# A fused transformer block, rebuilt: P as the stationary operand, scores over four row groups, engine lists from a planner

## Chip, cores, metric

One Trainium2 chip, one core. The metric is device time in microseconds (us), lower is better. A ratio compares a kernel's runs with those of the kernel before in the same rounds on the same chip, so it is not quite the ratio of the medians that are quoted. The kernel before ran in every set of rounds, with medians of 1544.6 to 1547.1 us, so medians of different sets can be compared to about 0.2%.

## The reference

Batch 1, 2048 tokens (S), width 1024 (D), 32 heads of 32 that share one K and one V, a gated FFN of width 3584, all inputs bf16:

```python
h  = x + softmax((LN(x) @ wq) @ (LN(x) @ wk).T / sqrt(32)) @ (LN(x) @ wv) @ wo   # per head; K and V shared
h2 = h + (sigmoid(LN(h) @ w_gate) * (LN(h) @ w_up)) @ w_down
```

The scores alone are 32 x 2048 x 2048 numbers, and each has to go through one exp on ScalarE (ACT).

## The kernel before

Queries are worked in 8 blocks of 256. Inside a block there are 8 quads of 4 heads, and for each quad 16 steps, one for each 128 keys. A step computes scores transposed (keys on partitions, 4 heads x 256 queries in two PSUM banks), ACT takes the exp of all 1024 columns, and P V accumulates with V and a block of ones as stationary operands over four column groups. The FFN of the block before is background work, put into fixed slots: two steps (a "unit" below) at a time.

Some words: P is the exp of the scores. A matmul's stationary operand (`lhsT`) is held in TensorE's 128x128 array while the other (`rhs`) moves past it. A row group is 32 of the array's rows, as many as a head is wide (`32*128` in the traces), and a column group 32 of its columns (`128*32`). Going from such a matmul to one over the whole array (`128*128`), or back, is a change of tiling. A PSUM bank holds 512 f32 columns; the program shares out eight of them.

```python
S_ps = psum_tensor("S_ps", [P, 4, 512])    # two score buffers of two banks
OL_ps = psum_tensor("OL_ps", [P, 2, 512])  # P V and row sums: two banks
F_ps = psum_tensor("F_ps", [P, 2, 512])    # all other matmuls: two banks
# ... cut ...
def quad_heads(q):                         # two tiles of Q^T, two row groups
    p_, lohi = q // 2, q % 2
    ta, tb = 2 * p_, 2 * p_ + 1
    rgx, rgy = (0, 1) if lohi == 0 else (2, 3)
    return [(ta, rgx), (tb, rgx), (ta, rgy), (tb, rgy)]

def pe_st(i):                              # scores of step i
    # ... waits cut, but for this one:
    if i >= 2: c_exp.wait(pe, i - 1)       # the buffer's exp, two steps ago
    for (j, bank, half) in [(0, 0, 0), (2, 1, 0), (1, 0, 1), (3, 1, 1)]:
        tile, rg = hq[j]
        pe.matmul(S_ps[:, 2 * buf + bank, half * QC:(half + 1) * QC],
                  lhsT=kT4[DH * rg:DH * (rg + 1), kt * P:(kt + 1) * P],
                  rhs=QT[DH * rg:DH * (rg + 1), tile, qc * QC:(qc + 1) * QC],
                  start=True, stop=True, tile_position=(DH * rg, 0))

def pe_pv(i):
    c_exp.wait(pe, i + 1)
    for j in range(4):                     # row sums
        pe.matmul(OL_ps[DH * j:DH * (j + 1), ob, QC:2 * QC], lhsT=ones,
                  rhs=Pring[:, slot, j * QC:(j + 1) * QC], tile_position=(0, DH * j), ...)
    for j in range(4):                     # V
        pe.matmul(OL_ps[DH * j:DH * (j + 1), ob, 0:QC], lhsT=V_sb[:, kt, :],
                  rhs=Pring[:, slot, j * QC:(j + 1) * QC], tile_position=(0, DH * j), ...)

# main loop, once in two steps (MACRO = 2); the exps of both steps stand on ACT
for i2 in range(jm - MACRO, jm):
    pe_pv(i2)
    if steps[i2][2] == KT - 1: dve_groupnorm(i2 // KT)
bg_step(cur_budget[0] * MACRO)             # FFN, projections: a fixed share of the block's work
for i2 in range(jm + MACRO, jm + 2 * MACRO):
    pe_st(i2)
```

The softmax here doesn't subtract the row's maximum and nothing guards it: scores larger than these inputs give would overflow.

## Time and profile before

| | before |
|---|---|
| median | 1544.52 us (3 runs, 1541.85 to 1546.78); a fourth, in the rounds with the kernel after, took 1552.20 |
| first exp starts, last exp ends | 64.0 us, 1426.4 us |
| behind the last exp | 118 us |
| distance of every second exp start (one unit): median, mean | 2.49 us, 2.66 us |

The page of the kernel before: busy time by engine, then busy tenths in 40 slices of the span.

```profile
span 1544.6 us, 38302 instructions
PE 1410.1 (91%) x17622; PEld 803.1 (52%) x17736; DVE 388.6 (25%) x686; ACT 1078.2 (70%) x1277; POOL 61.7 (4%) x117
...
PE   4799999999999999999999999999899999999678
...
ACT  2588886777687776877687776777688777777010
```

TensorE (PE) is busy in nearly every slice, ACT is not. The costliest groups of the same page (line, engine, operation, tiles, shapes, count, busy us, mean ns, idle time just before and who ended it):

```profile
L634 ACT ACTIVATE arena<-S_ps 128x1024 bf16<-128x1024 f32 x1024 | 1010.0, 1025 | 292.4 <-PE S_ps L624 291.5
...
L624 PE MATMUL S_ps<-arena 32*128 32x256 bf16 x4096 | 340.0, 280 | 22.9 <-ACT arena L634 20.7
L647 PE MATMUL OL_ps<-arena 128*32 128x256 bf16 x4096 | 275.1, 288 | 0.0
L653 PE MATMUL OL_ps<-arena 128*32 128x256 bf16 x4096 | 271.5, 285 | 0.0
```

ACT stands idle for 291.5 us because scores (L624) are not there. The timeline of one unit (start, duration, engine, line and so on; several instructions are merged in one line):

```profile
703.03 0.61 PE L624 MATMUL S_ps<-arena 32*128 32x256 bf16 x8
703.49 1.94 ACT L634 ACTIVATE arena<-S_ps 128x1024 bf16<-128x1024 f32 x2 [0.56 <-PE S_ps L624]
...
703.57 0.29 PE L647 MATMUL OL_ps<-arena 128*32 128x256 bf16 x4
...
703.69 0.28 PE L653 MATMUL OL_ps<-arena 128*32 128x256 bf16 x4
...
703.80 0.28 PE L647 MATMUL OL_ps<-arena 128*32 128x256 bf16 x4
...
703.91 0.28 PE L653 MATMUL OL_ps<-arena 128*32 128x256 bf16 x4
...
704.12 1.47 PE L274 MATMUL F_ps<-arena 128*128 128x512 bf16 x6
...
705.52 0.28 PE L624 MATMUL S_ps<-arena 32*128 32x256 bf16 x2
```

Read it as one turn of 2.49 us: scores at 703.03, two exps (1.94 us), P V, FFN, the next scores at 705.52. TensorE runs through, ACT waits 0.56 us a turn. A stretch of one block of 256 queries (busy time by engine, clock, share of DMA) says the same:

```profile
core 0: us, PE busy (x) PEld busy (x) DVE busy (x) ACT busy (x) POOL busy (x), PEclk, DMA share, GB/s
575.00:746.00 171.00, 160.56 (x2094) 92.58 (x2102) 39.97 (x67) 129.12 (x155) 3.06 (x6) 0.97 0.35 94
```

### The profile page before, as it was taken

The page shows a single profiled execution, that of the slowest core. Times are in us where ns is not written, and L with a number is a line of the kernel's source. Part 1 is how long each engine was busy: PE and PEld are TensorE (multiplying, and loading weights), DVE is VectorE, ACT ScalarE, POOL GpSimd, SP SyncE. Part 2 cuts the span into 40 slices and gives each one's busy share as a digit, 9 for nine tenths or more (in the row PEclk, how much of TensorE's full clock was granted, in tenths as well). Part 3 has the DMA queues.
Part 4 walks back from the last instruction along what each step waited for, and adds up shares of the span by engine and source line. Part 5 has one row for each costly group of instructions (what it writes and reads, how often), then busy time and mean ns, then how long its engine had stood idle before and what let it go on. Part 6 is the DMA issues. An engine that isn't in the chain of part 4 may idle for free.

```text
span 1544.6 us, 38302 instructions
## 1 busy us (share of the span) xinstructions
PE 1410.1 (91%) x17622; PEld 803.1 (52%) x17736; DVE 388.6 (25%) x686; ACT 1078.2 (70%) x1277; POOL 61.7 (4%) x117
## 2 busy tenths in 40 slices
PE   4799999999999999999999999999899999999678
PEld 2444336654466446654466445654466446654464
DVE  7433122211322123211322123211322123211311
ACT  2588886777687776877687776777688777777010
POOL 6200100000000000000000000000000000000000
PEclk9899768999899999999899999999899999999899
DMA  4500504550155204550155203550155204550371
GB/s 152 157 2 1 192 15 111 137 138 12 45 145 158 62 22 110 137 137 12 45 139 160 66 19 107 144 137 12 45 138 163 64 8 111 138 137 11 88 216 41
DMA packets 246417, 144.36 MB, mean 93 GB/s; under 512 B 5281, under 2 KB 238753, under 8 KB 246257
## 3 DMA queue, kind: packets, MB, share of 16 engines
q1 hardware_dynamic: 243712, 132.14, 31.1%
q0 software_dynamic: 2544, 9.77, 1.8%
q8 instruction: 139, 2.28, 0.6%
q14 instruction: 22, 0.17, 0.0%
HBM read 137.69 MB, written 4.19 MB: 92 GB/s over the span
## 4 chain that ended last, share of the span: by engine, by line
PE 74%; DMA 6%; DVE 6%; issue 6%; ACT 6%; POOL 1%; SPq 0%; POOLq 0%; DVEq 0%
PE F_ps L274 42%; PE S_ps L624 16%; PE OL_ps L647 8%; DMA arena<-in_B_w_up_dram 6%; PE OL_ps L653 6%; ACT arena L634 4%; DVE st L385 2%; DVE arena L844 2%; ACT tnh L839 2%; PE F_ps L446 1%; PE F_ps L520 1%; DVE arena L423 1%; POOL dsb L403 0%; DMA arena<-in_A_x_dram 0%; SPq L699 0%
## 5 line engine op out<-in xcount | busy, mean ns | idle before, releaser
L634 ACT ACTIVATE arena<-S_ps 128x1024 bf16<-128x1024 f32 x1024 | 1010.0, 1025 | 292.4 <-PE S_ps L624 291.5
L274 PE MATMUL F_ps<-arena 128*128 128x256 bf16 (+1 forms) x4866 | 778.2, 306 | 68.7 <-DVE arena L844 27.3
L274 PEld LDWEIGHTS F_ps<-arena 128*128 128x128 bf16 x4976 | 448.8, 99 | 335.0 <-issue 124.8
L624 PE MATMUL S_ps<-arena 32*128 32x256 bf16 x4096 | 340.0, 280 | 22.9 <-ACT arena L634 20.7
L647 PE MATMUL OL_ps<-arena 128*32 128x256 bf16 x4096 | 275.1, 288 | 0.0
L653 PE MATMUL OL_ps<-arena 128*32 128x256 bf16 x4096 | 271.5, 285 | 0.0
L624 PEld LDWEIGHTS S_ps<-arena 32*128 32x128 bf16 x4096 | 145.4, 93 | 223.4 <-ACT arena L634 150.8
L844 DVE SCALAR_TENSOR_TENSOR arena<-tnh,F_ps 128x256 bf16<-128x256 f32 x224 | 94.2, 421 | 618.6 <-ACT tnh L839 618.3
L647 PEld LDWEIGHTS OL_ps<-arena 128*32 128x32 bf16 x4096 | 109.7, 97 | 119.4 <-issue 115.7
L839 ACT ACTIVATE tnh<-F_ps 128x256 f32<-128x256 f32 x224 | 84.8, 379 | 105.8 <-PE F_ps L274 105.8
L667 DVE RECIPROCAL rL<-OL_ps 128x256 f32<-128x256 f32 x64 | 112.2, 1753 | 141.5 <-PE OL_ps L653 141.5
L653 PEld LDWEIGHTS OL_ps<-arena 128*32 128x32 bf16 x4096 | 111.6, 99 | 3.3
L886 DVE SCALAR_TENSOR_TENSOR arena<-F_ps,arena 128x512 bf16<-128x512 f32 x32 | 22.1, 691 | 209.5 <-PE F_ps L274 209.5
L446 PE MATMUL F_ps<-arena 128*128 128x128 bf16 x256 | 28.6, 280 | 39.5 <-DVE arena L423 38.9
L399 POOL TENSOR_SCALAR zb<-mvb 128x1 bf16<-128x1 bf16 x32 | 10.7, 334 | 1261.7 <-DVE mvr L394 1261.7
L446 PEld LDWEIGHTS F_ps<-arena 128*128 128x128 bf16 x256 | 21.4, 126 | 47.2 <-DVE arena L423 36.1
L741 DVE TENSOR_TENSOR arena<-F_ps,arena 128x512 bf16<-128x512 f32 x32 | 22.1, 691 | 87.9 <-PE F_ps L274 87.9
L385 DVE BATCH_NORM_STATS2 st<-arena 128x6 f32<-128x512 bf16 x64 | 40.9, 681 | 5.2 <-DMA arena<-in_A_x_dram 5.2
L504 DVE CAST arena<-F_ps 128x512 bf16<-128x512 f32 x30 | 20.7, 690 | 74.5 <-PE F_ps L274 71.0
L454 ACT ACTIVATE arena<-F_ps 128x1024 bf16<-128x1024 bf16 x16 | 16.1, 1025 | 27.2 <-PE F_ps L446 27.2
L672 DVE TENSOR_TENSOR arena<-OL_ps,rL 128x256 bf16<-128x256 f32 x64 | 27.1, 424 | 2.2
L403 POOL TENSOR_TENSOR dsb<-zb,smallb 128x1 bf16<-128x1 bf16 x32 | 23.2, 724 | 2.7
(30 smaller groups left out, 127.9 us busy)
## 6 DMA issues: line engine op xcount, KB each, us to landing
arena<-in_B_w_gate_dram SPq DMA_DIRECT2D x112, 512.0 KB, 3.9
arena<-in_B_w_up_dram SPq DMA_DIRECT2D x112, 512.0 KB, 5.3
arena<-in_A_x_dram SPq DMA_DIRECT2D x32, 256.0 KB, 2.7
arena<-in_B_w_down_dram POOLq DMA_DIRECT2D x4, 1792.0 KB, 16.2
out_dram<-arena SPq DMA_DIRECT2D x32, 128.0 KB, 1.7
arena<-in_A_wq_dram POOLq DMA_DIRECT2D x1, 2048.0 KB, 10.6
arena<-in_A_wo_dram SPq DMA_DIRECT2D x32, 64.0 KB, 1.9
arena<-in_A_wk_dram POOLq DMA_DIRECT2D x4, 64.0 KB, 4.2
```

Source lines behind the costliest of these rows:

```text
L274: last = pe.matmul(out_bank_ap, lhsT=lhsT, rhs=rhs, start=start, stop=stop)
L385: ins_ = dve.bn_stats(st[:, sslot, c, :], src[:, c * 512:(c + 1) * 512])
L403: ins_ = pool.tensor_tensor(out=dsb[:, t:t + 1], in0=zb[:, t:t + 1], in1=halfb_ap, op=ALU.pow)
L446: ins_ = pe.transpose(out=tpv[:, dt * P:(dt + 1) * P], in_=src[:, dt * P:(dt + 1) * P], identity=ident)
L624: ins_ = pe.matmul(S_ps[:, 2 * buf + bank, half * QC:(half + 1) * QC], lhsT=kT4[DH * rg:DH * (rg + 1), kt * P:(kt + 1) * P], rhs=QT[DH * r ...
L634: ins_ = act.activation(out=Pring[:, slot, :].rearrange("p (a b) -> p a b", a=2), in_=S_ps[:, 2 * buf:2 * buf + 2, :], func=ACTF.Exp, scal ...
L647: ins_ = pe.matmul(OL_ps[DH * j:DH * (j + 1), ob, QC:2 * QC], lhsT=ones, rhs=Pring[:, slot, j * QC:(j + 1) * QC], start=(kt == 0), stop=Fa ...
L653: ins_ = pe.matmul(OL_ps[DH * j:DH * (j + 1), ob, 0:QC], lhsT=V_sb[:, kt, :], rhs=Pring[:, slot, j * QC:(j + 1) * QC], start=False, stop=( ...
L667: ins_ = dve.reciprocal(rL[:, ob, :], OL_ps[:, ob, QC:2 * QC])
L672: ins_ = dve.tensor_tensor(out=OT[:, qc % 2, q, :], in0=OL_ps[:, ob, 0:QC], in1=rL[:, ob, :], op=ALU.mult)
L839: ins_ = act.activation(out=tnh[:, k % 2, :], in_=F_ps[:, b, 0:256], func=ACTF.Tanh, scale=0.5)
L844: ins_ = dve.scalar_tensor_tensor(out=hactT[:, ft, :], in0=tnh[:, k % 2, :], scalar=1.0, in1=F_ps[:, b, 256:512], op0=ALU.add, op1=ALU.mult)
```

## The change

The intent: take work from TensorE and keep ACT fed.

- P V: P becomes the stationary operand (128 keys x 128 queries), V and a ones column (33 columns) move past it. One group does all 16 key blocks of 4 heads in a row, so its output can share the two general banks, and the row-sum matmuls go.
- The two banks thus freed become a third score buffer (six banks).
- A score "visit" is 512 keys x 128 queries x 4 heads: 16 matmuls of 128 columns over four row groups, two exps behind it. It holds as many scores as a unit before, and there are 512 of both.
- A planner, run while the program is built, simulates the engines with assumed costs and fixes the order of each engine's list; FFN, projections and P V fill the time between visits.
- x is loaded whole and scores start with the first keys; the first layer norm (LN) centres on DVE and scales on DVE or ACT; Q goes through DRAM; four slabs of gate/up weights instead of two.

```diff
-        S_ps = EC(nc.psum_tensor("S_ps", [P, 4, 512], F32))
-        OL_ps = EC(nc.psum_tensor("OL_ps", [P, 2, 512], F32))
+        S_ps = EC(nc.psum_tensor("S_ps", [P, 6, 512], F32))
         F_ps = EC(nc.psum_tensor("F_ps", [P, 2, 512], F32))
@@ scores: pe_st() goes, emit_S() comes (cut) @@
+            deps = [q_ready[c][g], k_ev[2 * kq], k_ev[2 * kq + 1]]
+            if 2 * v - 2 >= 0:
+                deps.append(exps[2 * v - 2])
+            for kk in range(KB):
+                for j in range(4):
+                    kt = kq * KB + kk
+                    bank = 2 * ((2 * v + j // 2) % NB) + j % 2
+                    last = pl.op("pe", mm(S_ps[:, bank, kk * P:(kk + 1) * P], kT4[DH * j:DH * (j + 1), kt * P:(kt + 1) * P],
+                                          QTb[DH * j:DH * (j + 1), c % 2, g, qo:qo + P], True, True,
+                                          tile_position=(DH * j, 0)),
+                                 deps if (kk == 0 and j == 0) else [], occ=15.0, lat=15.0 + 170.0 + SEM)
@@ P V: pe_pv() goes, mk_PV() comes (cut) @@
+                for j in range(4):
+                    for kt in range(NT):
+                        r.append((mm(F_ps[:, b, j * VS:j * VS + DH + 1], Pr[:, slot, co:co + P], Vaug[:, kt, 0:DH + 1],
+                                     kt == 0, kt == NT - 1), DH + 1, []))
@@ the planner's choice (cut) @@
+                run = max(pl.free["act"], t) + sum(o.occ for o in pl.heap["act"])
+                can_s = sd is not None and known(sd, t)
+                if can_s and run - t < 750.0:
+                    emit_S(v)
@@ first LN (cut) @@
+            xcent[t] = pl.op("dve", lambda t=t: DVE.tensor_scalar(
+                out=x_sb[:, t, :], in0=x_sb[:, t, :], scalar1=mvr[:, 0, t, 0:1], scalar2=None, op0=ALU.subtract), ...)
+            xnorm[t] = evac(lambda: ACT.activation(out=dst, in_=src, func=ACTF.Copy, scale=sc),
+                            lambda: DVE.tensor_scalar(out=dst, in0=src, scalar1=sc, scalar2=None, op0=ALU.mult), ...)
```

## The prediction

> **What bounds the kernel now.** TensorE. Cut into eight windows of 171 us from 62 to 1430 us (busy time by windows), each has PE busy about 161 us (94%) and ACT about 130 us (76%). The timeline at 700 us shows the repeating unit, two score steps in 2.49 us: 8 score matmuls (about 0.54 us), 16 column-tiled P V and row-sum matmuls (about 0.55 us), FFN or projection matmuls (12 of 256 columns: 1.42 us, where 12 x 0.109 us = 1.3 us would do), and PE idle at three changes of array tiling (0.16 to 0.2 us where shown). ACT does two exps in 1.94 us and then waits 0.56 us for scores; one exp lasts 1.02 us, two in a row start 0.92 us apart. A window has 64 such units, so 2.67 us each with the larger stalls (output projection, layer norm, tanh to multiply).
> Outside: scores start at 63.6 us, after a first layer norm paced by DVE (2.76 us per tile); after the last exp (1426.4 us) comes 118 us, in which gate/up waits on weight DMA about 1 us for every slab (15 us), and 12 us go to projection and 6 us to norm bubbles.
>
> **What changes, per unit (512 in both).**
> - P V: P becomes the stationary operand, 33 columns move (V and a ones column), so the row-sum matmuls go. Still 16 matmuls. The V projection in the trace has this very form (128x128 weights, 32 columns): 32 in 0.95 us, 25 ns each when the clock is full. The Trainium skill, "TensorE: Matmul & The Clock Gate", Part 1, gives the same floor of about 25 ns. So 0.40 us instead of 0.55, and no column tiling, so one change of tiling fewer.
> - Scores: 16 matmuls of 128 columns over four row groups instead of 8 of 256 over two. Streaming halves (0.43 to 0.21 us), but weight loads double; with both changes of tiling I estimate 0.5 us. The skill's "TensorEngine Tiling" says a mode change drains the array; the trace's gaps agree.
> - FFN, projections, transposes: the same columns, about 82 us per 256 tokens, 1.28 us per unit.
> - Exps: the same 1024, ACT 1.84 us per unit, plus tanh about 0.12.
> - Removed: normalisation over 256 columns (reciprocal 1.75 us each), PE waits inside fixed slots; work is ordered by a planned list, three score buffers instead of two.
> - Head: x is loaded whole, scores start with the first keys (ACT idle worth about 30 us instead of 63). Tail: four weight slabs instead of two, about 95 us instead of 118.
>
> **Sum.** PE per unit 0.5 + 0.4 + 1.28 = 2.18 us, about 2.25 with stalls; ACT 1.96 us. PE still binds, ACT is close. Seven windows of 64 x 2.25 = 1008; the first, ACT-bound, 130; head 30; tail 92: about 1255 us.
>
> Prediction 1250 us, 80% range 1185 to 1350. Chances: faster by over 2% 0.96, within 2% 0.02, slower 0.02.
>
> **What would show each step right or wrong.** P V matmul starts 25 ns apart; a score visit, first to last matmul start and both drains, 0.45 to 0.6 us; distance of every second exp 2.2 to 2.3 us in mid-kernel, ACT over 80% busy; first exp before 25 us; last exp to the end 85 to 105 us.
>
> **What would make it wrong.** Score weight loads in four row groups that don't overlap (0.8 us per visit: over 1350). Planned times that miss the chip's, so the fixed orders make PE and ACT wait on each other (two PSUM banks now serve everything but scores). If scores cost 0.4 us and nothing stalls, ACT binds: about 1180.

## The result, and the profile after

The kernel after takes 1221.82 us (median of 4 runs, 1218.92 to 1225.61); the ratio to before is 0.7898, with a 95% interval of 0.7873 to 0.7924. That is 21% less time, and inside the predicted range.

| | before | after |
|---|---|---|
| first exp starts, last exp ends, us | 64.0, 1426.4 | 27.3, 1061.7 |
| behind the last exp, us | 118 | 162 |
| distance of every second exp, median, mean, us | 2.49, 2.66 | 1.89, 2.02 |

The page of the kernel after, the same lines:

```profile
span 1223.8 us, 47137 instructions
PE 1174.0 (96%) x22016; PEld 835.1 (68%) x22016; DVE 316.4 (26%) x838; ACT 1042.1 (85%) x1283; POOL 47.2 (4%) x109
...
PE   4899979999999999999999999999999999999999
...
ACT  6899999999999999999999999999999989711120
```

Now ACT is full too, from the first slices until the exps end. Its groups:

```profile
L495 ACT ACTIVATE Pr<-S_ps 128x1024 bf16<-128x1024 f32 x1024 | 972.4, 1052 | 26.4 <-PE S_ps L330 25.9
...
L330 PE MATMUL F_ps<-Vaug,Pr 128*128 128x33 bf16 x8192 | 244.4, 178 | 2.4 <-issue 1.5
L330 PE MATMUL S_ps<-QTb,kT 32*128 32x128 bf16 x8192 | 208.5, 218 | 15.4 <-ACT Pr L495 10.1
```

ACT's wait for scores went from 291.5 to 25.9 us. The timeline of two visits in mid-kernel:

```profile
601.71 5.78 ACT L495 ACTIVATE Pr<-S_ps 128x1024 bf16<-128x1024 f32 x6
...
602.23 0.40 PE L330 MATMUL S_ps<-QTb,kT 32*128 32x128 bf16 x16
...
602.56 1.69 PE L330 MATMUL F_ps<-zone,hact 128*128 128x512 bf16 x7
...
604.18 0.40 PE L330 MATMUL S_ps<-QTb,kT 32*128 32x128 bf16 x16
...
604.51 1.47 PE L330 MATMUL F_ps<-zone,hact 128*128 128x512 bf16 x6
```

Six exps run without a gap over three visits, since the scores for the next pair are made while an exp of the pair before still runs. A stretch of mid-kernel:

```profile
core 0: us, PE busy (x) PEld busy (x) DVE busy (x) ACT busy (x) POOL busy (x), PEclk, DMA share, GB/s
584.00:715.00 131.00, 127.92 (x2615) 90.81 (x2613) 29.01 (x80) 125.88 (x153) 2.68 (x6) 0.99 0.37 103
```

Both engines are over 95% busy. What TensorE does not get done under the exps is left behind them. This is its timeline there; the last exp ends at 1061.7 us:

```profile
1074.47 47.32 PE L330 MATMUL F_ps<-hnT,ring 128*128 128x256 bf16 x432
1121.63 0.61 PE L619 MATMUL F_ps<-ident,hn 128*128 128x128 bf16 x8
1123.02 0.62 PE L619 MATMUL F_ps<-ident,hn 128*128 128x128 bf16 x8 [0.79 <-DVE hnT L625]
1123.48 24.34 PE L330 MATMUL F_ps<-zone,hact 128*128 128x512 bf16 x112
1147.65 49.07 PE L330 MATMUL F_ps<-hnT,ring 128*128 128x256 bf16 x448
1196.56 24.34 PE L330 MATMUL F_ps<-zone,hact 128*128 128x512 bf16 x112
```

The whole FFN of the seventh block waits there, ahead of that of the eighth: all 448 of its gate/up matmuls start after the last exp, 432 of them in the first line.

A ledger of TensorE, worked out from the start times of all matmuls in the two traces: the time from each start to the next start is booked to the first of the two, so waits and changes of tiling are in it.

| us | before | after | difference |
|---|---|---|---|
| scores, with the change of tiling behind them | 323 | 191 | -132 |
| P V (before: and row sums), with what follows | 343 | 222 | -121 |
| everything else, with waits | 866 | 798 | -68 |

It adds up to the difference of the spans, 1544.6 to 1223.8 us. It looks like a proof that cheaper matmul forms gave most of the gain. It isn't one: a ledger says where time is booked, not what would happen if one entry changed alone. The experiments ask that.

### The profile page after: what moved, and what is told of

Its sections match the earlier page's. It is cut to its first block, busy times and chain, and to the rows that moved or that the text cites. A ratio compares the mean times of both kernels' runs of the same rounds, so it can differ in the third digit from the quotient of the medians.

```text
span 1223.8 us, 47137 instructions
## 1 busy us (share of the span) xinstructions
PE 1174.0 (96%) x22016; PEld 835.1 (68%) x22016; DVE 316.4 (26%) x838; ACT 1042.1 (85%) x1283; POOL 47.2 (4%) x109
## 4 chain that ended last, share of the span: by engine, by line
PE 63%; ACT 31%; issue 3%; DVE 2%; POOL 0%; DMA 0%
PE F_ps L330 54%; ACT Pr L495 28%; PE S_ps L330 9%; ACT tnh L669 1%; ACT zone L313 1%; PE F_ps L619 0%; ACT zone L230 0%; DVE OT L566 0%; DVE st L274 0%; DVE st L276 0%; PE F_ps L558 0%; DMA ring<-in_A_x_dram 0%; POOL dsb L287 0%; DVE hnT L625 0%; DVE ring L307 0%
## 5 line engine op out<-in xcount | busy, mean ns | idle before, releaser
L495 ACT ACTIVATE Pr<-S_ps 128x1024 bf16<-128x1024 f32 x1024 | 972.4, 1052 | 26.4 <-PE S_ps L330 25.9
L330 PE MATMUL F_ps<-hnT,ring 128*128 128x256 bf16 x3584 | 440.6, 275 | 2.5 <-DVE OT L566 1.2
L330 PEld LDWEIGHTS F_ps<-hnT,ring 128*128 128x128 bf16 x3584 | 332.5, 98 | 61.3 <-issue 3.1
L330 PEld LDWEIGHTS F_ps<-Vaug,Pr 128*128 128x128 bf16 x8192 | 229.7, 96 | 28.1 <-issue 4.1
L330 PE MATMUL F_ps<-Vaug,Pr 128*128 128x33 bf16 x8192 | 244.4, 178 | 2.4 <-issue 1.5
L330 PE MATMUL S_ps<-QTb,kT 32*128 32x128 bf16 x8192 | 208.5, 218 | 15.4 <-ACT Pr L495 10.1
L330 PE MATMUL F_ps<-zone,hact 128*128 128x512 bf16 x896 | 213.2, 380 | 0.8 <-DVE OT L566 0.5
L330 PEld LDWEIGHTS S_ps<-QTb,kT 32*128 32x128 bf16 x8192 | 119.2, 93 | 127.9 <-ACT Pr L495 81.6
L676 DVE SCALAR_TENSOR_TENSOR hact<-tnh,F_ps 128x256 bf16<-128x256 f32 x224 | 94.3, 421 | 384.0 <-ACT tnh L669 383.9
L330 PEld LDWEIGHTS F_ps<-zone,hact 128*128 128x128 bf16 x896 | 79.2, 98 | 91.3 <-DVE OT L566 0.7
```

The lines of the kernel that those rows point to most:

```text
L330: return lambda: PE.matmul(o, lhsT=l, rhs=r, start=start, stop=stop, **kw)
L495: exps[u] = pl.op("act", lambda slot=slot, pb=pb: ACT.activation(out=Pr[:, slot, :].rearrange("p (a b) -> p a b", a=2), in_=S_ps[:, pb:pb ...
L676: e = pl.op("dve", lambda: DVE.scalar_tensor_tensor(out=hactT[:, ft, :], in0=tnh[:, k, :], scalar=1.0, in1=F_ps[:, b, 256:512], op0=ALU.ad ...
```

## The experiments

### The two matmul forms, put into the kernel before

Is the gain in the forms? Two theories stood against each other: that the time is the sum of TensorE's work, and that exps and scores form a ring which cheaper matmuls do not shorten.

`b_pv`: only P V. The result is brought back by two transposes a group; it is correct.

```diff
-    pe.matmul(OL_ps[DH*j:DH*(j+1), ob, QC:2*QC], lhsT=ones, rhs=Pring[:, slot, j*QC:(j+1)*QC], ...)
-    pe.matmul(OL_ps[DH*j:DH*(j+1), ob, 0:QC], lhsT=V_sb[:, kt, :], rhs=Pring[:, slot, j*QC:(j+1)*QC], ...)
+    for hf in range(2):                                  # k8 = 4 * hf + j
+        pe.matmul(OL_ps[:, ob, k8*34:k8*34+33], lhsT=Pring[:, slot, j*QC+hf*P:j*QC+(hf+1)*P], rhs=Vaug[:, kt, 0:33], ...)
```

> The kernel before, with only P V changed: P stationary, 33 columns of V and ones moving, plus the two transposes per group that bring the result back; correct result. Work theory (the time before is the sum of what TensorE executes, so cheaper matmul forms alone give the gain): a unit of two score steps loses 0.575 - 0.40 = 0.17 us of TensorE, 512 units, so about 90 us less, 1450 to 1470 us. Ring theory (with two score buffers, handed over in pairs, a unit cannot be shorter than two exps, 1.94 us, plus the 0.56 us until new scores are there, about 2.5 us, whatever TensorE saves): 0 to 30 us less, 1515 to 1545 us, and TensorE now waits for exps before the scores.

Measured: 1504.99 us, ratio 0.9726 (0.9692 to 0.976), 42 us less. The median unit fell from 2.49 to 2.36 us, nearly as the work theory has it, so this kernel was not held by a ring at 2.5 us. But of the 84 us that leave the P V row of the ledger (343 to 259), about half come back in the others: score pairs now wait for an exp (+17 us), and the rest takes 28 us more, 9 of them the added transposes and 19 waits. Neither theory fits.

`b_rg`: only the scores. All four heads of a quad come from one tile of Q, and the two steps of a unit are made together, so that four row groups write four banks. (Each group gets a bank of its own: the Trainium skill, "TensorEngine Tiling (Array Packing)", under "Restrictions and Gotchas", says that different row tiles cannot access the same PSUM bank at the same time; no run here tried it.) P V keeps its form, but is regrouped to match, both steps behind both exps.

```diff
-    return [(ta, rgx), (tb, rgx), (ta, rgy), (tb, rgy)]
+    return [(q, 0), (q, 1), (q, 2), (q, 3)]
-    if i >= 2: c_exp.wait(pe, i - 1)      # step by step
+    if i >= 2: c_exp.wait(pe, i)          # both steps at once
+    for (k2, j) in [(k2, j) for k2 in range(2) for j in range(4)]:
+        pe.matmul(S_ps[:, j, k2*QC:(k2+1)*QC], lhsT=kT4[DH*j:DH*(j+1), (kt+k2)*P:(kt+k2+1)*P], rhs=QT[DH*j:DH*(j+1), q, ...], ...)
```

> The kernel before, with only the scores changed: 8 matmuls of 256 columns over four row groups and four banks instead of two and two; correct result. Work theory: scores with the change of tiling after them fall from 0.62 to about 0.34 us a unit, 512 units, so about 145 us less, about 1400 us. Ring theory: the exps still wait for the pair of buffers; at most 0.05 us a unit less, 1515 to 1545 us.

Measured: 1592.29 us, ratio 1.0285 (1.0261 to 1.031): 45 us slower, outside both. From the first score matmul to the next other matmul it takes 0.33 us instead of 0.54, as wanted. But four row groups need four banks at once, which is all there is: the scores can only start when both exps of the pair before have ended.

`b_both`: both forms.

> Both changes of matmul form in the kernel before, its fixed slots and two score buffers kept. Work theory: about 235 us less, about 1310 us. Ring theory: 1500 to 1545 us, TensorE busy share well down, ACT still idle about 0.5 us after every pair of exps.

Measured: 1584.66 us, ratio 1.0243 (1.0221 to 1.0264), above both ranges: 37 us slower with 165 us less of busy TensorE (1410.1 to 1245.1 us). Its timeline:

```profile
702.30 0.40 PE L621 MATMUL S_ps<-arena 32*128 32x256 bf16 x8 [0.43 <-ACT arena L631]
...
702.79 1.94 ACT L631 ACTIVATE arena<-S_ps 128x1024 bf16<-128x1024 f32 x2 [0.54 <-PE S_ps L621]
703.05 1.47 PE L273 MATMUL F_ps<-arena 128*128 128x256 bf16 x12
...
704.78 0.40 PE L621 MATMUL S_ps<-arena 32*128 32x256 bf16 x8 [0.27 <-ACT arena L631]
...
705.27 1.03 ACT L631 ACTIVATE arena<-S_ps 128x1024 bf16<-128x1024 f32 x1 [0.54 <-PE S_ps L621]
```

That is a closed ring: two exps (1.94 us), then 0.54 us for the scores of the next pair, 2.48 us whatever else TensorE saves. TensorE waits for exps (0.43 and 0.27 us here) and ACT for scores (0.54 us) in the same turn. P V in its cheap form is worth 8 us in this ring (1592 to 1585).

### The third score buffer, taken away after

`a_nb2`: the kernel after, planned anew, with two score buffers.

```diff
-    NB = 3
+    NB = 2
-    deps.append(exps[2 * v - 2])
+    deps.append(exps[2 * v - 1])
```

> The kernel after, planned as it is, but with two score buffers (four banks) instead of three (six banks). Work theory: TensorE does the same work, 1220 to 1250 us. Ring theory: a visit becomes two exps (1.87 us) plus 0.5 to 0.6 us until new scores are there, 2.4 to 2.5 us, 512 visits, plus 27 us head and about 97 us tail: 1350 to 1410 us.

Measured: 1520.32 us, ratio 0.9819 (0.9793 to 0.9845), against 0.7898 with three buffers: 298 us in the medians. The ring theory has the direction right and the size too low: the median visit is 2.66 us, not 2.4 to 2.5. The timeline:

```profile
703.28 0.61 PE L330 MATMUL S_ps<-QTb,kT 32*128 32x128 bf16 x16
...
703.95 1.94 ACT L495 ACTIVATE Pr<-S_ps 128x1024 bf16<-128x1024 f32 x2 [0.72 <-PE S_ps L330]
...
705.94 0.61 PE L330 MATMUL S_ps<-QTb,kT 32*128 32x128 bf16 x16 [2.05 <-ACT Pr L495]
706.61 1.94 ACT L495 ACTIVATE Pr<-S_ps 128x1024 bf16<-128x1024 f32 x2 [0.72 <-PE S_ps L330]
```

Two exps and 0.72 us. The gap is longer than in `b_both`, and here a visit's score matmuls last 0.61 us instead of 0.40. TensorE had stood still for 2.05 us before those at 705.94, and its mean granted clock over this run is 0.877 against 0.993 with three buffers.

Such visits, with slow scores, are 133 of 511. In the others the scores run at full pace, but in most of them TensorE still has other work of its list to do when the exps end (here at 510.82 us):

```profile
508.43 0.40 PE L330 MATMUL S_ps<-QTb,kT 32*128 32x128 bf16 x16
508.76 2.55 PE L330 MATMUL F_ps<-zone,hact 128*128 128x512 bf16 x11
508.88 1.94 ACT L495 ACTIVATE Pr<-S_ps 128x1024 bf16<-128x1024 f32 x2 [0.78 <-PE S_ps L330]
...
511.25 0.40 PE L330 MATMUL S_ps<-QTb,kT 32*128 32x128 bf16 x16
...
511.70 1.02 ACT L495 ACTIVATE Pr<-S_ps 128x1024 bf16<-128x1024 f32 x1 [0.88 <-PE S_ps L330]
```

In 334 visits the scores follow other matmuls without a pause and start 0.26 us (median) after the end of the exps; in `b_both` the median of all is 0.055 us. So the 298 us are not the ring's alone. An estimate: with the 2.48 us turn of `b_both` in all 512 visits, and this run's 28 us before and 94 us behind, the time would be about 1390 us. About 170 us would then be the ring's, and about 130 us come from how this list meets two buffers.

So the parts of the change hang together. P as the stationary operand, with a whole group done in a row, frees two banks. They become the third buffer. With it, scores that need four banks at once no longer stop the exps. Without it, the cheap P V alone brought 42 us, and both cheap forms together lost 37.

### What sets the time once three buffers are there

Two equal doses, one for each engine, each known to the planner, and a plain rule instead of the planned moment of a visit.

`a_actdose`:

```diff
+    dose.append(pl.op("act", lambda: ACT.activation(out=adose[:, v % 8, :], in_=ident[:, 0:64], func=ACTF.Copy), ..., **t_act(64)))
```

> The kernel after with one small extra ACT instruction (a copy of 128x64 into a scratch tile) in each of the 512 visits, planned for; about 0.12 us each, 62 us of ACT in all. Work theory: scores end some 60 us later, but the FFN backlog behind the last exp (162 us, of which about 97 us are the last 256 tokens) shrinks as much: 0 to 15 us more, 1222 to 1237 us. ACT theory: about 60 us more, 1280 us.

`a_pedose`:

```diff
-    r = []
+    r = [(mm(F_ps[:, b, 384:512], ident[:, :], ident[:, :], True, True), P, []) for _ in range(8)]
```

> The kernel after with 8 idle matmuls of 128 columns (56 ns each) ahead of each of the 128 P V groups, 57 us of TensorE in all, planned for; results unchanged. Work theory: about 57 us more, 1275 to 1285 us. ACT theory: 0 to 20 us more.

`a_fixed`:

```diff
-    if can_s and run - t < 750.0:
+    if can_s and since >= 1600.0:        # nominal ns of other matmuls since the last visit
```

> The kernel after with a plain rule in place of the planned moment of a score visit: the next visit goes in once 1.6 us of other matmuls are listed since the last one (and its data are there), not when ACT is about to run dry. Work theory: the order hardly matters as long as TensorE is not idle: 1215 to 1250 us, the backlog after the last exp smaller. If instead the planned moment is what makes the kernel fast: over 1290 us.

| | median, us | ratio (95%) | last exp ends, us | behind it, us |
|---|---|---|---|---|
| after | 1221.82 | 0.7898 (0.7873 to 0.7924) | 1061.7 | 162 |
| `a_actdose` | 1228.94 | 0.7948 (0.792 to 0.7975) | 1115.3 | 112 |
| `a_pedose` | 1276.61 | 0.8254 (0.823 to 0.8278) | 1056.3 | 218 |
| `a_fixed` | 1233.36 | 0.7974 (0.7952 to 0.7997) | 1114.8 | 116 |

The dose on TensorE costs 55 us of the 57 put in. The dose on ACT moves the last exp by 54 us and the end by 7: what TensorE could not do under the exps it would have done behind them anyway. (A larger dose on ACT, which would use up that backlog, was not tried.) `a_fixed` spreads the same work otherwise, ends its exps 53 us later too and loses 12 us. So after the change TensorE's work sets the time, ACT paces only the scores, and the planned moment of a visit is worth about 1%. The work theory, which failed for the kernel before, holds here.

### Which row groups, and in which order

`a_rg2` and `a_rg1` reorder a visit's 16 score matmuls; everything else is kept.

```diff
 # a_rg2
-    for kk in range(KB):
-        for j in range(4):
+    for jj, kk in [(jj, kk) for jj in (0, 2) for kk in range(KB)]:
+        for j in (jj, jj + 1):
 # a_rg1
-    for kk in range(KB):
-        for j in range(4):
+    for j in range(4):
+        for kk in range(KB):
```

> The kernel after with one thing undone: a visit's 16 score matmuls are ordered so that only two row groups work at a time (heads 0 and 1 over all keys, then heads 2 and 3); lists, buffers and counts as they are. Work theory (after, with three buffers, the sum of TensorE's work sets the time): the score matmuls take 0.21 to about 0.43 us more or less as in the kernel before, so 0.2 us more in each of 512 visits, about 110 us more, about 1330 us. ACT theory (after, the exps set the time and TensorE has room): at most 30 us more.

Measured: 1231.85 us, ratio 0.7965 (0.7942 to 0.7989), 10 us more. Since the dose had shown that TensorE's time counts in full, the scores cannot have taken 0.2 us longer. The starts in the trace agree: the block grew from 0.335 to 0.355 us a visit, 0.02 us x 512 = 10 us.

> The kernel after with a visit's 16 score matmuls in the order of heads: four in row group 0, four in group 1, and so on. After the run with two row groups at a time, which cost 10 us only. Row-group theory (a row group takes one column a cycle, so what counts is how many groups stream at once; the pairs were cheap for another reason): a visit's scores take about 0.85 us instead of 0.21, over 1450 us. Size theory (score matmuls of 128 columns start about 14 ns apart whatever their row group, and the gain came from halving them): under 1260 us.

Measured: 1237.22 us, ratio 0.7995 (0.7972 to 0.8017), 15 us more, with a block of 0.365 us.

`b_n128` asks whether the size of the matmuls did it: each score matmul of the kernel before is cut in two.

```diff
-    for (j, bank, half) in order:
+    for (pair, hc) in [(0, 0), (0, 1), (1, 0), (1, 1)]:
+        for (j, bank, half) in order[2 * pair:2 * pair + 2]:   # columns half * QC + hc * P, 128 of them
```

> The kernel before with each score matmul of 256 columns cut in two of 128, order and row groups (two at a time) kept; correct result. Row-group theory: the same streaming time, 1535 to 1560 us. Size theory: the score block from first start to the next matmul falls from 0.54 to about 0.36 us, 0.18 us in each of 512 units, half of it lost to waits as with P V: 1450 to 1505 us.

Measured: 1548.61 us, ratio 1.001 (0.998 to 1.004), no change, with a block of 0.549 us. The size theory of `a_rg1` falls with it.

`b_orders` then put eight orders side by side in one kernel, one for each quad of heads.

> A measurement, not a faster kernel (it hands two buffers over in pairs, about 1600 us; correct result): the kernel before with the same score work in eight orders, one for each quad of heads, read from the trace as the time from the first score matmul to the next other matmul. 256 columns: A four row groups in turn; B two groups at a time, keys changing every second matmul; C one group at a time, two key blocks each. 128 columns: D two groups at a time, the same keys for two query halves in a row; E two groups, keys changing, queries kept; F four groups in turn; G one group, keys changing; H one group, keys kept for both halves. Row-group theory (a group takes one column a cycle): A, F 0.33 us; B, D, E 0.54; C, G, H about 1.0. New-weights theory (a matmul overlaps the one before it in its row group if it brings other keys, as in all runs of the kernel after, and not if it brings the same ones, as in the kernel before): A, B, C, E, F, G 0.33 to 0.40; D and H longer, 0.45 to 1.0.

Measured: 1671.55 us (one run, state unknown; only durations inside the trace are used). Median from the first score matmul to the next other matmul, 64 blocks each, worked out from the starts:

| order | A | B | C | D | E | F | G | H |
|---|---|---|---|---|---|---|---|---|
| us | 0.328 | 0.334 | 0.337 | 0.356 | 0.356 | 0.332 | 0.367 | 0.367 |

Both theories fail: even C and H, listed one group at a time, are nearly as fast (0.337 and 0.367 us, where about 1.0 and at least 0.45 were expected). The reason can be read from which matmuls raise a semaphore, which the trace records with each. In G and H every second matmul of the program's order has one. In the order of their starts this is one block of H (start in ns from the first, + raises a semaphore):

```
0-  13-  30-  44-  65+  80+  96+  110+  121-  135-  152-  166-  177+  191+  208+  222+
```

In the order of the list the signs would alternate. They come four without, then four with, in all 128 blocks of G and H. The trace does not name the row group, but the one reading that fits is that the first matmul of each of the four row groups starts, then the second of each: TensorE takes matmuls of other row groups ahead of their place in the list. So the order in the list is nearly free, and what counts is over how many row groups the work in reach is spread. In the kernel before a unit uses only two, in a visit four. The closest pair is D and `b_n128`: both list matmuls of 128 columns two groups at a time over four banks, but D has four groups in its block and `b_n128` two, and they take 0.356 and 0.549 us. The other runs of this section and `b_rg` fit too; how far TensorE reaches ahead was not measured.

### The first layer norm

`a_ln1fused`: one DVE instruction a tile, as in the second layer norm.

```diff
-    xcent[t] = ... DVE.tensor_scalar(... op0=ALU.subtract)
-    xnorm[t] = evac(... ACT.activation(... scale=sc), ... DVE.tensor_scalar(... op0=ALU.mult))
+    xnorm[t] = norm(0, t, x_sb[:, t, :], xn[:, t % 2, :], sv1[t], deps, 1)
```

> The kernel after with the first layer norm in one DVE step a tile (subtract and multiply, without rounding in between) instead of centring on DVE and scaling on DVE or ACT. Only the first 60 us can change. If the two steps help by giving half of the scaling to ACT: 2 to 8 us slower. If ACT, which also evacuates there, is what holds the head up: 2 to 8 us faster.

Measured: 1222.47 us, ratio 0.79 (0.7875 to 0.7924), the same time, and a result that fails the comparison with the reference (relative error 0.0227). Neither expectation holds for the time. The head did get shorter: the first exp starts at 22.5 us instead of 27.3, but nothing of it arrives at the end. The run shows that the result needs the two steps, or at least not this fused one; the rounding of the centred x between them is the likely reason, but no run separated it.

## Why the prediction was right, and where not

**The bound after.** "PE still binds, ACT is close" holds: 55 of 57 us of a TensorE dose arrive at the end, 7 of an ACT dose of about the same size.

**P V.** 25 ns a matmul was read from the V projection of the trace before, and it came: the median start-to-start distance of the 8192 P V matmuls is 25 ns. The floor that the Trainium skill gives in "TensorE: Matmul & The Clock Gate" (Part 1) agrees.

**Scores.** Put at 0.5 us a visit with both changes of tiling, with 0.45 to 0.6 as the sign to look for. Measured: 0.335 us to the next matmul plus 0.096 us for the change of tiling before it, 0.43 us. This and the stalls (0.07 us a unit expected) are the terms that were sized too high. Between the first and the last exp, the other matmuls stand further apart than undisturbed ones of their size (56, 109 and 216 ns) by 61 us in all before, and by 20 us after, 0.04 us a unit. The reason given, streaming over four row groups, stands, but not the order of the list that seemed to do it.

**The shape of the time.** Wrong in three signs. Every second exp comes after 1.89 us (median), not 2.2 to 2.3: scores run at the pace of ACT and leave TensorE's other work behind. So behind the last exp stand 162 us, not 85 to 105. And the first exp starts at 27.3 us, not before 25. The two large misses cancel in the sum, because it is TensorE's work that is summed either way.

**What the prediction left out.** It costed the parts one by one ("So 0.40 us instead of 0.55", "Streaming halves") and set no worth on "three score buffers instead of two". The sum came because all parts were there, but the parts do not earn their own terms. In the kernel before, the two forms give -42 us (P V), +45 us (scores) and +37 us together. In the kernel after, taking the third buffer away costs 298 us, an estimated 170 of them by the ring. On the way from 1547 us (before, in these rounds), both forms lead to 1585, the rest of the rebuild without the third buffer to 1520, and the third buffer to 1222. That is one way through the parts; another would share them out otherwise.

**What stays open.** How the 64 us between `b_both` and `a_nb2` divide into the earlier start, the weight slabs and the lists was not measured. Two buffers handed over one at a time in the planned kernel were not tried, nor a list tuned to two buffers, nor the two forms with a third buffer but without the planner.

## What to carry to other kernels

Before counting what a cheaper instruction saves, draw the ring it sits in: which buffers are handed over together, and what the engine on the other side does meanwhile. A form that needs all buffers at once can be slower though it is cheaper, and a form that frees memory for one more buffer can be worth more than the time that it saves itself. To learn which engine sets the time when two are over 95% busy, give each a small known dose and see which one arrives at the end.

## What the Trainium skill lacked or had wrong

- "TensorE: Matmul & The Clock Gate", Part 3, says of matmuls that they are "strict FIFO, no reordering", and Part 2 that only weight loads are pulled ahead. The trace of `b_orders` shows matmuls starting before earlier ones of the list (the pattern of semaphores in orders G and H, read above as other row groups going ahead), and 16 matmuls listed one row group after the other take 0.367 us, against 0.332 us listed in turn.
- The same page, Part 2, "Back-to-back issue gap", gives sustained 81 ns at 128 and 131 ns at 512 columns for streams with a weight load each, and calls the formula N / 2.4 + 2.5 one for isolated matmuls. In these traces, with a weight load each, the median distances are 56 ns (128 columns), 109 ns (256) and 216 ns (512): the formula.
- "TensorEngine Tiling (Array Packing)", "Key Properties", says that a change of tiling mode drains the array; no page gives the cost. Here a score matmul after a 256-column full-array matmul starts 205 ns after it where the next of the same kind starts after 109, so 96 ns more; the way back costs about as much (147 ns after a matmul of 128 columns where 56 would do, so 91).
- The same page, "Restrictions and Gotchas", says that different row tiles write to different PSUM banks. No page says what follows for a kernel that has to overlap such scores with exps: 1520 us with four banks for scores, 1222 us with six.
